# Strassen for the first channel product of eight of nine chunks, with a bank that is seeded by a copy

## The chip, the cores and the metric

The kernel runs on one core of one Trainium2 chip. A core has five engines that run side by side, each through its own instructions in order: TensorE (PE in the profile, its weight loads PEld), VectorE (DVE), ScalarE (ACT), GpSimd (POOL) and SyncE (SP). TensorE multiplies a stationary operand of 128x128 with a moving one and writes into PSUM, eight banks of 128 partitions x 512 float32. DVE and ACT read and write PSUM and the on-chip memory SBUF; POOL works on SBUF alone. DMA queues bring data in and out; POOL's queue also converts types, SP's also transposes. The metric is the device time of one run in microseconds (us).

## The reference

Eight sequences (b) of 576 rows and 8 heads of 64 go through an attention of exponential features, then through a mixer of two products over the rows ("token") and two over the columns ("channel"):

```python
h = x @ omega.T - sum(x*x)/2;  phi = exp(h - max(h)) / sqrt(128)      # for q and k
x = (phi_q @ (phi_k.T @ v)) / (phi_q @ sum(phi_k) + 1e-6)             # per b and head
u = x + (relu(x.T @ w_tok1) @ w_tok2).T                               # 576 -> 256 -> 576
out = u + relu(u @ w_ch1) @ w_ch2                                     # 512 -> 1536 -> 512
```

The matrices on chip are float16, sums are float32, the output is float32.

## The kernel before, in words

The rows of each sequence are split: the first 512 form one chunk, c = 0 to 7, and the last 64 rows of all eight sequences together form chunk 8. Each sequence passes through attention (`attention`), token products (`token_mix`, for the first sequence `token_mix_first`, and `token_tail` for the last rows of two sequences) and a DMA transpose of u to `uT`. Then `channel_mix` works on the chunk. Its first product takes the weights `wc1` (512 x 1536, held as 4 blocks of depth by 12 column blocks) as stationary operand and `uT` as moving one: for each of the 12 column blocks four matmuls of 512 columns into one bank (line 967), and a relu out of the bank into `r3` in float16, by ACT or DVE (lines 290 and 292).

The second product of chunks 1 to 8 is done by Strassen's scheme in Winograd's form (`channel_out_fast`): both factors are cut into 2x2 quarters, and seven products of quarters replace eight. Sums and differences of the weight quarters are made once (`T1` to `T4`, line 448), those of `r3` for each chunk (the sums S, eight DVE instructions of 128x768 a chunk, line 295). The seven products, each 12 matmuls of 256 columns (line 917), accumulate in three banks, X, Y and Z. DVE reads them out (`read`, line 906): the first product (bank X) is read twice in effect, once to u + X into the output tile `o`, and Y is then added to that.

The sequence of everything is fixed. The code makes a list of jobs, each with its engine; `ORDER` says in which order the jobs are issued, `SLOT` which of the rings' buffers or banks each takes, `MOVED` which jobs go to another engine than the usual one. An engine takes its instructions strictly in that order, with semaphores for what it needs from others. Negative entries of `ORDER` are idle matmuls at the start. So attention of later sequences is interleaved by the list with channel products of earlier chunks.

Loads of sequences 2 to 7 go in two steps: POOL's queue casts q and k to float16 into a scratch in DRAM, SP's queue brings them back transposed into rings `qT` and `kT`; v comes by POOL's queue into the ring `v`. Each of these rings has three buffers. POOL otherwise scales v (`vs`, line 295) and the tails of v (`vbd`).

## Time and profile before

| | before |
|---|---|
| time, median of 3 runs | 283.24 us (282.99 to 283.85) |
| span of the profiled execution | 281.1 us |
| TensorE busy | 270.3 us, 96% |
| VectorE busy | 222.4 us, 79% |
| ScalarE busy | 138.6 us, 49% |
| GpSimd busy | 92.0 us, 33% |

The span runs from the first to the last instruction of one profiled execution; the page gives no other time for it. In the rows of groups stand line, engine and operation, the tile written and the tiles read with partitions x elements and type, and how often; behind the bar the busy time in us and the mean length of one in ns, then the idle time of the engine ahead of them with who ended it. Matmuls overlap, so the busy time of PE is more than the time in which its array works; the pitch of a row of matmuls without a gap is read from the chain instead. In the rows of stretches stand the bounds, the length, and the busy time of PE, PEld, DVE, ACT and POOL, with the number of instructions, the granted clock and the share of the DMA engines.

### The profile page before, as it was taken

To read this page: it belongs to the slowest core of one execution; us is meant where nothing else is said; L and a number is where in the kernel's file an instruction comes from. 1 tells how busy PE (TensorE), PEld (TensorE's weight loads), DVE (VectorE), ACT (ScalarE), POOL (GpSimd) and SP (SyncE) were. 2 spreads that over 40 slices of the span, in tenths; PEclk is the share of its full clock that TensorE was granted. 3 is DMA by queue.
4 is the path that set the end of the run, shared out by engine and by line. 5 is a ranking of instruction groups with operands and counts; after the bars stand their busy time and mean duration, and the time that the engine had idled before them with its cause. 6 is when DMAs were issued, how large, how long until landed. Compare 5 with 4: busy or idle time off the path is not lost.

```text
span 281.1 us, 6278 instructions
## 1 busy us (share of the span) xinstructions
PE 270.3 (96%) x2526; PEld 167.6 (60%) x2526; DVE 222.4 (79%) x462; ACT 138.6 (49%) x288; POOL 92.0 (33%) x116
## 2 busy tenths in 40 slices
PE   6899999999999999999999999999999999999993
PEld 2547546443657755665667647755676467446782
DVE  2589828499999899996997999977995893565992
ACT  1498994049676418743758445734753510031200
POOL 8574994007510872048008710510033000000001
PEclk9999999999999999999999999999999999999999
DMA  6999999999998999997979993960151304030125
GB/s 161 194 189 161 157 169 213 178 191 202 179 218 184 148 172 186 181 198 104 212 178 185 241 135 101 161 156 2 76 97 59 111 0 96 0 149 2 75 90 135
DMA packets 80524, 39.66 MB, mean 141 GB/s; under 512 B 63984, under 2 KB 76016, under 8 KB 80304
## 3 DMA queue, kind: packets, MB, share of 16 engines
q0 software_dynamic: 31744, 17.74, 44.1%
q1 hardware_dynamic: 46832, 15.77, 29.1%
q10 hardware_dynamic: 1920, 5.77, 5.4%
q8 instruction: 19, 0.31, 0.4%
q14 instruction: 9, 0.07, 0.1%
HBM read 35.95 MB, written 16.52 MB: 187 GB/s over the span
## 4 chain that ended last, share of the span: by engine, by line
PE 89%; DVE 3%; DMA 2%; ACT 2%; issue 0%; SPq 0%; DVEq 0%
PE bank L967 32%; PE bank L917 26%; PE bank L791 5%; PE bank L778 5%; PE bank L1001 4%; PE bank L735 3%; PE bank L657 3%; PE bank L702 3%; DMA wc<-in_k_dram 2%; PE bank L669 2%; ACT kp L515 1%; PE bank L845 1%; PE bank L817 1%; PE bank L737 1%; PE bank L771 1%; DVE T L448 1%
## 5 line engine op out<-in xcount | busy, mean ns | idle before, releaser
L967 PE MATMUL bank<-uT,wc 128*128 128x512 f16 x376 | 89.6, 379 | 0.5 <-DVE r L292 0.4
L290 ACT ACTIVATE r<-bank 128x512 f16<-128x512 f32 (+1 forms) x86 | 47.7, 601 | 82.7 <-PE bank L967 61.5
L295 POOL TENSOR_TENSOR vs<-v,vs 128x512 f16<-128x512 f16 x32 | 34.2, 1072 | 94.4 <-DVE vs L683 51.3
L967 PEld LDWEIGHTS <-wc 128*128 128x128 f16 x424 | 38.8, 98 | 38.8 <-issue 1.6
L917 PEld LDWEIGHTS <-r 128*128 128x128 f16 x384 | 36.8, 98 | 8.2 <-issue 1.1
L515 ACT ACTIVATE kp<-bank 128x512 f16<-128x512 f32 x64 | 36.7, 618 | 8.9 <-PE bank L657 7.1
L515 ACT ACTIVATE qp<-bank 128x512 f16<-128x512 f32 x64 | 36.7, 614 | 8.8 <-PE bank L669 5.8
L681 DVE TENSOR_REDUCE km<-kp 128x8 f16<-128x1024 f16 x32 | 38.7, 1208 | 1.2 <-ACT kp L515 1.1
L292 DVE TENSOR_SCALAR r<-bank 128x512 f16<-128x512 f32 (+1 forms) x40 | 26.3, 670 | 15.7 <-PE bank L967 11.3
L745 DVE TENSOR_TENSOR x<-bank,rc 128x320 f16<-128x320 f32 x62 | 30.5, 492 | 2.1
L917 PEld LDWEIGHTS <-S 128*128 128x128 f16 x288 | 28.1, 98 | 5.8 <-issue 0.3
L906 DVE TENSOR_TENSOR o<-u,bank 128x512 f32<-128x512 f16 x28 | 19.0, 679 | 6.2 <-PE bank L917 5.8
L917 PE MATMUL bank<-T,r 128*128 128x256 f16 x192 | 23.8, 273 | 0.0
L917 PE MATMUL bank<-wc,r 128*128 128x256 f16 x192 | 23.6, 273 | 0.0
L917 PE MATMUL bank<-T,S 128*128 128x256 f16 x192 | 23.4, 273 | 0.0
L946 POOL DMA_DIRECT2D out_dram<-o x2 | 1.3, 645 | 61.2 <-issue 61.2
L906 DVE TENSOR_TENSOR o<-o,bank 128x512 f32<-128x512 f32 (+1 forms) x27 | 16.6, 617 | 2.5 <-PE bank L917 1.8
L735 PEld LDWEIGHTS <-qp 128*128 128x128 f16 x256 | 13.5, 98 | 8.1 <-DVE kvsb L286 0.7
L794 DVE TENSOR_TENSOR u<-x,bank 128x512 f16<-128x512 f16 x28 | 17.6, 680 | 0.0
L735 PE MATMUL bank<-kvsb,qp 128*128 128x65 f16 x256 | 15.0, 193 | 0.5 <-DVE kvsb L286 0.5
L791 PE MATMUL bank<-r,w 128*128 128x512 f16 x56 | 14.1, 381 | 0.0
L744 DVE RECIPROCAL rc<-bank 128x5 f32<-128x5 f32 x62 | 11.4, 184 | 2.9 <-PE bank L737 2.2
(119 smaller groups left out, 379.0 us busy)
## 6 DMA issues: line engine op xcount, KB each, us to landing
out_dram<-o ACTq DMA_DIRECT2D x9, 512.0 KB, 2.7
q<-in_q_dram POOLq DMA_DIRECT2D x6, 576.0 KB, 9.7
wc<-in_moe_w_ch_dram POOLq DMA_DIRECT2D x4, 768.0 KB, 9.0
k<-in_k_dram POOLq DMA_DIRECT2D x6, 512.0 KB, 7.8
v<-in_v_dram POOLq DMA_DIRECT2D x6, 512.0 KB, 9.9
out_dram<-o SPq DMA_DIRECT2D x5, 512.0 KB, 3.9
r<-in_q_dram POOLq DMA_DIRECT2D x4, 288.0 KB, 7.5
v<-in_v_dram POOLq DMA_DIRECT2D x4, 256.0 KB, 8.1
```

Of the source, the lines that this page charges most:

```text
L290: nc.scalar.activation(out=out, in_=in_, func=AF.Relu)
L292: nc.vector.tensor_relu(out=out, in_=in_)
L295: (nc.gpsimd if eng == "POOL" else nc.vector).tensor_tensor(**kw)
L515: nc.scalar.activation(out=out, in_=in_, func=AF.Exp, bias=0.0, scale=1.0)
L681: nc.vector.reduce_max(out=mx, in_=kpv, axis=AX.X)
L735: nc.tensor.matmul(ps[:, k, j * 65 : (j + 1) * 65], st, s[:, i, 0 : D + 1], start=True, stop=True)
L745: nc.vector.tensor_tensor(out=t_x[place("x", b)][:, :, (2 * hp + hs[0]) * D : (2 * hp + hs[0] + n) * D].rearrange("p j (i d) -> p i j d", ...
L791: nc.tensor.matmul(ps, w2_of(tb, j), r1[:, tb, :], start=(tb == 0), stop=(tb == NT - 1))
L794: nc.vector.tensor_tensor(out=t_u[place("u", b)][:, j, :], in0=t_x[place("x", b)][:, j, :], in1=bank(n), op=ALU.add)
L906: nc.vector.tensor_tensor(out=o, in0=a, in1=ps, op=ALU.add)
L917: nc.tensor.matmul(ps[:, j * DH : (j + 1) * DH], a[:, cb, j * P : (j + 1) * P], w[:, cb, :], start=(bank_of(b, j0) not in held and j == j0 ...
L967: nc.tensor.matmul(ps, wc1[:, db, cb * P : (cb + 1) * P], moving(db), start=(db == 0), stop=(db == ND - 1))
```

## The change

The first channel product of chunks 1 to 8 is done by Strassen's scheme too (`channel_in_fast`). Sums of quarters of `wc1` are made once (`first_weights`: three in a new tile `t_W`, one in place), four sums of quarters of `uT` for each chunk (tile `t_V`, one in place). The 1536 columns are worked in three pairs p of column blocks of both halves. For each pair seven products of four matmuls of 256 columns go into banks X, Y and Z: product 1 into X, then a copy of bank X into bank Y by ACT or DVE, on which product 2 is accumulated; products 6, 7 and 4 go on into X. X is copied out after 6 and after 7 (kept copies `t_s`, float32). Two quarters of the result come straight from a bank with a relu, the other two are the sum of a kept copy and bank Z, written by DVE, and get their relu in place in SBUF (two parts each).

In the second product of chunks 1 to 7, bank X is likewise copied to bank Y behind the first product, and the second is accumulated there; one DVE read falls away per chunk. Matmuls on a seeded bank have no start flag; the list sees to it that the bank's last user wrote all of it.

The rings `qT`, `kT` and `v` go from three buffers to two, `qp` and `kp` from four to three. `T3` and one sum of `wc1` overwrite a quarter of the weights, behind the plain products of chunk 0. `ORDER`, `SLOT` and `MOVED` are new throughout. In them, of the sums S 35 of 64 go to POOL, of the 32 input sums 20, of the eight weight sums three; more jobs have a second engine to choose from. The second product's weights are loaded later, behind the casts of sequence 2.

```diff
-    COUNT = {"qT": 3, "kT": 3, "v": 3, "vt": 2, "qp": 4, "kp": 4, "vs": 4, "qpt": 2, "kpt": 2, "vbd": 2,
-             "kvsb": 3, "ktt": 2, "x": 3, "r1": 3, "u": 3, "uT": 3, "r3": 2, "S": 1, "o": 2, "bank": 8}
+    COUNT = {"qT": 2, "kT": 2, "v": 2, "vt": 2, "qp": 3, "kp": 3, "vs": 4, "qpt": 2, "kpt": 2, "vbd": 2,
+             "kvsb": 3, "ktt": 2, "x": 3, "r1": 3, "u": 3, "uT": 3, "V": 1, "s": 4, "r3": 2, "S": 1, "o": 2, "bank": 8}
...
-    t_T = sb([P, 4, NH, DH], FP16, "T")
+    t_T = sb([P, 3, NH, DH], FP16, "T")
+    t_W = sb([P, 3, 2, NH * P], FP16, "W")
...
+    t_V = ring(COUNT["V"], [P, 3, 2, 2, P], FP16, "V")
+    t_s = ring(COUNT["s"], [P, 512], FP32, "s")
...
+    def second_weights(plain):
+
+        for out_, a, b in ((T1, W12, W11), (T2, W22, T1), (T4, W21, T2), (T3, W22, W12)):
+            e_w = engine("DVE", "POOL")
+            def go_w2(o=out_, a=a, b=b, e_w=e_w):
+                tt(e_w, out=o, in0=a, in1=b, op=ALU.subtract)
+            j_T.append(add(e_w, 0.95, KEYS["T"], go_w2, deps=[*j_wc2, *j_T[-1:], *j_vbd_users, *(plain if b is W12 else [])]))
+
+    A11, A21, A12, A22 = [wc1[:, 2 * k : 2 * k + 2, e * NH * P : (e + 1) * NH * P] for k in range(2) for e in range(2)]
+    S1, S2, S4 = [t_W[:, i] for i in range(3)]
+    S3 = A21
+    j_W = {}
+
+    def first_weights(plain):
+
+        for n, out_, a, b, op in ((1, S1, A21, A22, ALU.add), (2, S2, S1, A11, ALU.subtract), (4, S4, A12, S2, ALU.subtract), (3, S3, A11, A21, ALU.subtract)):
+            e_w = engine("DVE", "POOL")
+            def go_w1(o=out_, a=a, b=b, op=op, e_w=e_w):
+                tt(e_w, out=o, in0=a, in1=b, op=op)
+            j_W[n] = add(e_w, 0.95, KEYS["T"] - 0.2, go_w1, deps=[*j_wc1, *([j_W[n // 2]] if n in (2, 4) else [*j_W.values()]), *(plain if n == 3 else [])])
...
+    PARTS = (slice(0, 4), slice(4, NH))
...
-            prev = []
-            for k, (i, what, op) in enumerate(steps):
-                e_sum = engine("DVE")
-                def go(what=what, op=op, part=part, e_sum=e_sum, c=c, g=g, k=k):
+            for k, (i, what, op, need, after) in enumerate(steps):
+                e_sum = engine("DVE", "POOL")
+                def go_s(what=what, op=op, part=part, e_sum=e_sum, c=c):
                     o, a, b = what()
                     tt(e_sum, out=o[:, part], in0=a[:, part], in1=b[:, part], op=op)
-                job = add(e_sum, 0.5, key + KEYS["S"] + 0.1 * g + 0.01 * k, go, deps=[*need, *prev], take=[("S", c)])
-                prev = [job]
+                job = add(e_sum, (0.61, 0.34)[g], key + KEYS["S"] + 0.1 * g + 0.01 * k, go_s,
+                          deps=[*need, *[sums[x][g] for x in after], *j_early_users], take=[("S", c)])
                 sums.setdefault(i, []).append(job)
...
-                                             start=(bank_of(b, j0) not in held and j == j0 and cb == 0), stop=False, skip_group_check=True)
+                                             start=(bank_of(b, j0) not in held and j == j0 and cb == 0 and (tail or k != 1)), stop=False, skip_group_check=True)
...
-                if k == 0:
+                if k == 0 and tail:
                     outs["sA", h] = read(k, "X", 0, 0, True, [j], False, j0, j1)
+                elif k == 0:
+                    e_a = engine("ACT", "DVE")
+                    def go_a(e_a=e_a):
+                        copy(e_a, bank(bank_of("Y", 0)), bank(bank_of("X", 0)))
+                    outs["sA", h] = add(e_a, 0.5, key + KEYS["c2"], go_a, deps=[j], take=[("bank", bank_of("Y", 0))])
                 elif k == 1:
-                    outs["11", h] = read(k, "Y", 0, 0, False, [j, outs["sA", h]], True, j0, j1)
+                    outs["11", h] = read(k, "Y", 0, 0, not tail, [j, outs["sA", h]], True, j0, j1)
...
+    def channel_in_fast(c, key, jt):
+        def src():
+            return t_uT[place("uT", c)] if c < B else uTt
+        def u_of(k, i):
+            return src()[:, 2 * i : 2 * i + 2, 2 * k : 2 * k + 2, :]
+        def v_of(n):
+            return t_V[place("V", c)][:, n]
+        own = [("uT", c)] if c < B else []
+        first = [tr[x] for x in tr if c < NPE and x[1] == c]
+        sums = {}
+        for n, what, op, after in (
+            (1, lambda: (v_of(0), u_of(0, 1), u_of(0, 0)), ALU.subtract, ()),
+            (2, lambda: (v_of(1), u_of(1, 1), v_of(0)), ALU.subtract, (1,)),
+            (4, lambda: (v_of(2), u_of(1, 0), v_of(1)), ALU.subtract, (2,)),
+            (3, lambda: (u_of(0, 1), u_of(1, 1), u_of(0, 1)), ALU.subtract, (1,)),
+        ):
+            e_sum = engine("POOL", "DVE")
+            def go_u(what=what, op=op, e_sum=e_sum):
+                o, a, b = what()
+                tt(e_sum, out=o, in0=a, in1=b, op=op)
+            sums[n] = add(e_sum, 1.0, key - 0.2, go_u, deps=[*jt, *[sums[x] for x in after]], take=[("V", c)], give=own)
+        ops = {
+            1: ("X", A11, lambda: u_of(0, 0), [], True), 2: ("Y", A12, lambda: u_of(1, 0), [], False),
+            6: ("X", S2, lambda: v_of(1), [sums[2], j_W[2]], False), 5: ("Z", S1, lambda: v_of(0), [sums[1], j_W[1]], True),
+            7: ("X", S3, lambda: u_of(0, 1), [sums[3], j_W[3]], False), 3: ("Z", S4, lambda: u_of(1, 1), [j_W[4]], False),
+            4: ("X", A22, lambda: v_of(2), [sums[4]], False),
+        }
+        raw = {(i, e): [] for i in range(2) for e in range(2)}
+        for p in range(NH // 2):
+            at = key + 0.15 * p
+            def bank_of(b, p=p):
+                return ("c" + b, c, p)
+            def rows(i, e, p=p):
+                return t_r3[place("r3", c)][:, NH * e + 2 * p : NH * e + 2 * p + 2, 2 * P * i : 2 * P * i + 2 * P]
+            def seen(b, bank_of=bank_of):
+                return bank(bank_of(b)).rearrange("p (t s) -> p t s", t=2)
+            def product(n, deps, give=(), p=p, bank_of=bank_of, at=at):
+                b, a, moving, need, begin = ops[n]
+                def go_p(b=b, a=a, moving=moving, begin=begin):
+                    ps, m = bank(bank_of(b)), moving()
+                    for t in range(2):
+                        cb = 2 * p + t
+                        for k in range(2):
+                            nc.tensor.matmul(ps[:, 2 * P * t : 2 * P * t + 2 * P], a[:, k, cb * P : (cb + 1) * P], m[:, :, k, :],
+                                             start=(begin and t == 0 and k == 0), stop=False, skip_group_check=True)
+                j = add("PE", mm(4, 256), at, go_p, deps=[*jt, *j_wc1, *first, *need, *deps], take=[("bank", bank_of(b)), ("r3", c)],
+                        give=[*([("V", c)] if n in (4, 5, 6) else own), *give])
+                j.heavy = True
+                return j
+            def kept(x, deps, give=(), p=p, seen=seen, at=at):
+                e_k = engine("ACT", "DVE")
+                def go_k():
+                    copy(e_k, t_s[place("s", (c, p, x))].rearrange("p (t s) -> p t s", t=2), seen("X"))
+                return add(e_k, 0.5, at, go_k, deps=deps, take=[("s", (c, p, x))], give=give)
+            def summed(x, b, i, e, deps, free, p=p, seen=seen, rows=rows, at=at, bank_of=bank_of):
+                def go_t():
+                    nc.vector.tensor_tensor(out=rows(i, e), in0=t_s[place("s", (c, p, x))].rearrange("p (t s) -> p t s", t=2), in1=seen(b), op=ALU.add)
+                j = add("DVE", 0.6, at, go_t, deps=deps, give=[("s", (c, p, x))] + ([("bank", bank_of(b))] if free else []))
+                raw[i, e].append(j)
+                return j
+            p1 = product(1, [])
+            e_a = engine("ACT", "DVE")
+            def go_a(e_a=e_a, bank_of=bank_of):
+                copy(e_a, bank(bank_of("Y")), bank(bank_of("X")))
+            ka = add(e_a, 0.5, at, go_a, deps=[p1], take=[("bank", bank_of("Y"))])
+            p2 = product(2, [ka])
+            p5 = product(5, [])
+            e_y = engine("ACT", "DVE")
+            def go_y(e_y=e_y, rows=rows, seen=seen):
+                relu_to(e_y, rows(0, 0), seen("Y"))
+            raw[0, 0].append(add(e_y, 0.5, at, go_y, deps=[p2], give=[("bank", bank_of("Y"))]))
+            p6 = product(6, [ka])
+            kb = kept("b", [p6])
+            p7 = product(7, [kb])
+            kc = kept("c", [p7])
+            t22 = summed("c", "Z", 1, 1, [kc, p5], False)
+            p3 = product(3, [t22])
+            summed("b", "Z", 1, 0, [kb, p3], True)
+            p4 = product(4, [kc])
+            e_r = engine("ACT", "DVE")
+            def go_r(e_r=e_r, rows=rows, seen=seen):
+                relu_to(e_r, rows(0, 1), seen("X"))
+            raw[0, 1].append(add(e_r, 0.5, at, go_r, deps=[p4], give=[("bank", bank_of("X"))]))
+        ready = {k: [raw[k][:2], raw[k][2:]] for k in ((0, 0), (0, 1))}
+        for i, e in ((1, 1), (1, 0)):
+            ready[i, e] = []
+            for g, part in enumerate(PARTS):
+                e_p = engine("DVE", "ACT")
+                def go_n(part=part, i=i, e=e, e_p=e_p):
+                    x = t_r3[place("r3", c)][:, NH * e + part.start : NH * e + part.stop, 2 * P * i : 2 * P * i + 2 * P]
+                    relu_to(e_p, x, x)
+                ready[i, e].append([add(e_p, (0.33, 0.2)[g], key + 0.4, go_n, deps=raw[i, e][2 * g : 2 * g + 2])])
+        return ready
...
     def channel_mix(c, key, jt):
+        if c == NPE - 1:
+            first_weights(j_plain["in"])
+            second_weights(j_plain["out"])
+        if c >= NPE - 1:
+            channel_out_fast(c, key, channel_in_fast(c, key, jt))
+            return
         def moving(db):
```

147 lines of the change are left out of this document (81 added, 66 removed), and 110 rows, old and new, of the table ORDER.

## The prediction

> **What bounds the kernel now.** I read the page first, then the busy time by stretch, the chain in order of time, who waited for whom, and last the groups of instructions for prices.
>
> ```profile
> span 281.1 us, 6278 instructions
> PE 270.3 (96%) x2526; PEld 167.6 (60%) x2526; DVE 222.4 (79%) x462; ACT 138.6 (49%) x288; POOL 92.0 (33%) x116
> PE 89%; DVE 3%; DMA 2%; ACT 2%; issue 0%; SPq 0%; DVEq 0%
> DMA  6999999999998999997979993960151304030125
> ```
>
> The median of the runs is 283.24 us, 2.1 us above this span; I count gains in the span and take them off the median. TensorE (PE) holds 89% of the chain. The DMA engines are full up to about slice 26 (183 us).
>
> ```profile
> 67.00:281.10 214.10, 208.57 (x1868) 133.89 (x1864) 176.59 (x360) 97.29 (x197) 52.29 (x61) 1.00 0.68 127
> 67.00:209.00 142.00, 141.59 (x1363) 89.89 (x1360) 127.99 (x264) 83.70 (x171) 47.01 (x56) 1.00 0.90 157
> 67.00:95.00 28.00, 27.59 (x277) 17.72 (x274) 26.33 (x52) 19.14 (x40) 9.45 (x12) 1.00 1.04 182
> PE bank L967 <- DVE r L292: 0.4, 1, 0.4
> PE bank L771 <- DVE x L745: 0.3, 1, 0.3
> ```
>
> Chunk 1's first product begins near 67 us. The first three rows give, after the length, busy PE, weight loads, DVE, ACT and POOL; from there to the end PE is covered, and the last two rows are all that it waited for (0.7 us). DVE is busy 127.99 of 142 us (90%) up to 209 us and 26.33 of 28 (94%) in the fullest stretch, still without holding PE up. So two limits lie close together: PE, which the change unloads, and DVE, which it loads.
>
> **The change part by part. PE.**
>
> ```profile
> 229.29 5.24 PE bank L917 x48
> 238.88 13.81 PE bank L967 x64
> L917 PEld LDWEIGHTS <-r 128*128 128x128 f16 x384 | 36.8, 98 | 8.2 <-issue 1.1
> ```
>
> Back to back, a 512-column matmul of the first product takes 13.81/64 = 215.8 ns, and a 256-column one, the form that all new products have, 5.24/48 = 109.2 ns. A chunk's first product goes from 48 x 0.2158 = 10.36 us to 84 x 0.1092 = 9.17 us: 1.19 us, for eight chunks 9.5 us. The bank copy adds nothing on PE. The weight load of 98 ns still fits under 109. In the Trainium skill, "TensorE: Matmul & The Clock Gate", section "Back-to-back issue gap", a sustained stream is put at about 81 ns for 128 columns and 131 ns for 512; by that (an estimate, 98 ns for 256 columns) the plain form would take 6.3 us and the new one 8.2, a loss. The rows above contradict it at both widths, and the rows decide.
>
> **DVE, ACT and POOL.** Prices (mean ns in the second place behind the bar):
>
> ```profile
> L290 ACT ACTIVATE r<-bank 128x512 f16<-128x512 f32 (+1 forms) x86 | 47.7, 601 | 82.7 <-PE bank L967 61.5 <-PE bank L778 11.4 <-DVE o L906 5.4
> L292 DVE TENSOR_SCALAR r<-bank 128x512 f16<-128x512 f32 (+1 forms) x40 | 26.3, 670 | 15.7 <-PE bank L967 11.3 <-PE bank L778 3.6 <-PE bank L552 0.5
> L906 DVE TENSOR_TENSOR o<-o,bank 128x512 f32<-128x512 f32 (+1 forms) x27 | 16.6, 617 | 2.5 <-PE bank L917 1.8 <-issue 0.3
> L286 DVE COPY o<-bank 128x512 f32<-128x512 f32 x2 | 1.4, 686 | 0.2 <-PE bank L1001 0.2
> L286 ACT COPY o<-bank 128x512 f32<-128x512 f32 x2 | 1.2, 602 | 1.4 <-PE bank L1001 1.4
> L295 DVE TENSOR_TENSOR S<-r 128x768 f16<-128x768 f16 x16 | 8.8, 551 | 0.6 <-ACT r L290 0.4
> L295 POOL TENSOR_TENSOR vs<-v,vs 128x512 f16<-128x512 f16 x32 | 34.2, 1072 | 94.4 <-DVE vs L683 51.3 <-PE bank L669 22.2 <-PE bank L917 13.8
> L295 POOL TENSOR_TENSOR vbd<-vt,vbd 128x512 f16<-128x512 f16 x6 | 6.3, 1053 | 20.4 <-DVE vbd L594 17.7 <-DMA vt<-in_v_dram 2.6
> L295 POOL TENSOR_TENSOR T<-vt,T 128x1024 f16<-128x1024 f16 x1 | 1.9, 1937 | 0.0
> 20.22 1.07 POOL L295 TENSOR_TENSOR vs<-v,vs 128x512 f16<-128x512 f16 x1
> 20.62 0.83 DVE L631 COPY qpt<-qpt 128x512 f16<-128x512 f16 x1 [0.49 <-ACT qpt L515]
> 64.51 0.91 DVE L448 TENSOR_TENSOR T<-wc,T 128x1536 f16<-128x1536 f16 x1
> 64.85 1.48 POOL L295 TENSOR_TENSOR vs<-v,vs 128x512 f16<-128x512 f16 x1
> 65.33 1.81 DVE L448 TENSOR_TENSOR T<-wc 128x1536 f16<-128x1536 f16 x1
> 71.05 1.07 POOL L295 TENSOR_TENSOR vs<-v,vs 128x512 f16<-128x512 f16 x1
> 71.13 1.82 DVE L448 TENSOR_TENSOR T<-wc,T 128x1536 f16<-128x1536 f16 x1
> ```
>
> I counted the jobs of both lists by engine (the order in which the code makes jobs, with the table of moved ones). DVE loses 35 of 64 sums S (x 0.551 = 19.3 us), 20 of 40 relus out of a bank (x 0.670 = 13.4), 7 reads of the second product (x 0.617 = 4.3) and six small copies (0.3 to 0.8 each, 4.3): 41.3 us. It gains 48 sums of a kept product and a bank (nearest row L906, 0.617): 29.6; 13 bank or kept copies (0.686): 8.9; 12 sums of 512 elements over the chunk's input, by the slope from 768 elements at 0.551 to 1536 at 0.91, 0.43 each: 5.2; 17 in-place relus; a fifth weight sum, 0.9; and five value products from POOL, 2.4. For an in-place relu the nearest row is the copy within SBUF at 20.62: 0.83 us, of which it stood 0.67 behind a POOL product that ended at 21.29, so 0.16 alone. Between 0.16 and 0.83 I take 0.3, since half its length was standing still and the first parts are twice as long: 5.1. Net 52.1 - 41.3 = +11 us, nearly all behind 67 us: 176.6 + 11 = 188 us.
>
> ACT gains 27 bank copies and 39 kept copies (x 0.602 = 39.7), loses 28 relus (x 0.601 = 16.8) and gets 15 in-place relus (0.6 for 512 elements, up to 1.0): some 13. From 138.6 us to about 175, 64% of the new span: never the bound, but now four times in the bank X of every product pair. The list puts at least 0.8 us of other PE work between a product and the next that needs its copy (the least of 24 pairs; the middle ones have 1.3 to 3.3), against a copy of 0.60. I cost the bank copies at nothing, covered by that work; without cover each would cost PE 0.6 us. A product that waits for its copy holds every later group in PE's queue, attention's too, and the copy stands in ACT's queue behind the exponentials. Behind the last attention only channel products are left; there chunks 7 and 8 cover each other's copies, at least 0.87 us in the list.
>
> POOL gains 35 sums S (17 of 1024 elements x 1.937, 18 of 512 x 1.072), 20 input sums (1.072) and three weight sums (1.5 x 1.937 each): 82 us, so about 170 with what it hands over, 63%. Work on two operands is then 119 us, 44% of the new span. POOL's queue also issues all casting loads, so a load now stands behind sums that wait for the transposed input.
>
> What DVE and POOL do to each other is the unknown. Where two such instructions meet in the rows above, one stands still: the weight sum alone took 0.91 us, and 1.81 and 1.82 beside a POOL product; the product at 64.85 took 1.48 and not 1.07. The Trainium skill says it so in "SBUF — State Buffer", section "Who interferes with whom": a VectorE instruction with two SBUF inputs, or in a two-port mode, and a GpSimd instruction that reads SBUF hold a shared port, and the loser blocks fully. The trace agrees: 0.9 us lost by DVE per meeting. It speaks against the change, which puts far more of both kinds on these engines.
>
> ```profile
> L295 DVE TENSOR_TENSOR S<-r x16: 547/551/559, 80.7 to 266.5; 128x768 f16<-128x768 f16 x16
> ```
>
> (Minimum, median, maximum: the sums S never met one; by chance about 64 x 16% = 10 would have, POOL's products of before being 32 x 1.072 + 6 x 1.053 + 2 x 1.94 = 44.5 us of 281.) After the change 68 DVE instructions are of this kind. DVE standing still holds the reads that free banks, and PE behind them. At random 44% of them, 30, would start inside a POOL sum and stand for half of its mean 1.28 us: 19 us. Laid apart as S was, none. I take a third, 6 us, nearer to the row that shows none, but there is less room to lie apart: 188 + 6 = 194 us on DVE. Filled to 93%, about what the fullest stretch shows, that takes 208.6 us where PE alone needs 214.1 - 9.5 = 204.6. So DVE decides: gain 5.5 us.
>
> **Loads.** Rings for q, k and v shrink from three to two.
>
> ```profile
> 175.54 3.23 SPq L380 DMA_TRANSPOSE kT<-k  x1
> 202.16 0.62 PE L657 MATMUL bank<-omT,kT 64*128 64x128 f16 x16
> 60.55 0.12 PEld L552 LDWEIGHTS <-kT 64*128 64x128 f16 x4 [0.48 <-DMA kT<-k]
> q0 software_dynamic: 31744, 17.74, 44.1%
> wc<-in_moe_w_ch_dram POOLq DMA_DIRECT2D x4, 768.0 KB, 9.0
> kT<-k SPq DMA_TRANSPOSE x6, 6.8
> ```
>
> The last batch's k is fetched 26 us ahead of its main use: two buffers at a distance of a chunk (142 us over five, about 28) suffice and cost nothing; with that cover gone each batch would wait up to the 6.8 us of a transpose. Batch 2 is different. PE waited for it already (0.48 us), and the new list puts it 18 us of PE work earlier. Ahead of it the second product's weights (two loads of 768 KB) have gone; at the casting queue's 17.74 MB in 183 us they are worth 16 us. It comes 2 us late, or at the outside between 2 us early and 4 late; since PE's part before it also has gaps to give, I take 1 us. The head's other reordering, the new slots and the store queues moved from SP to ACT (their issue is not on the chain) I cost at nothing, inside the same bounds. The tail's stores are as before.
>
> Sum: 283.24 - 5.5 + 1.0 = 278.7 us.
>
> **The rivals.** *Full gain*: sums and POOL work lie apart, DVE 188/0.93 = 202 us stays under PE's 204.6: 283.24 - 9.5 = 273.7. For it: 0.7 us of PE waits with DVE at 90%. Against it: POOL's share goes from 16% to 44%.
>
> *DVE and POOL in each other's way, slower*: the random 19 us gives (188 + 19)/0.93 = 222.6, 8.5 us more than 214.1: 291.7. It tips to slower from about 12 us of standing still: (188 + 12)/0.93 = 215. For it: three of the four weight sums met a product, two stood still. Against it: S, none of 64.
>
> *Loads late*: batch 2, or a cast held up in POOL's queue, keeps PE waiting 10 us instead of 1: 283.24 - 9.5 + 10 + the 1 to 2 us of a jammed restart, 285.
>
> *Narrow matmuls slower than wide ones per column*, by the TensorE page's figures 283.24 + 8 x 1.9 = 298 (an estimate from that page). As a mechanism of rows: 84 weight loads x 98 ns = 8.2 us, under 9.17, so loads do not bind. Chance under 1 in 100.
>
> **How the numbers follow.** Below 275.5, full gain and a head that gets shorter: 0.17. The forecast, 275.5 to 282.4: 0.42. Within 0.3%, about what a measurement of this kernel can tell from no change (282.4 to 284.1): 0.05. DVE and POOL: 0.26. Loads or head late: 0.10. Hence faster 0.59, same 0.05, slower 0.36. The likeliest case by itself spans 275.5 to 282; the range reaches to 272.5, the full gain with a us from the head, and to 290, most of the slower cases.
>
> **What would show it.** Steps right: the first product's line gives way to 84 matmuls of 256 columns per chunk at 109 ns; DVE near 188 us behind 67 us plus what its SBUF sums grew by; PE waiting some 4 us for DVE, in rows that name sums, kept copies or the in-place relus. Sums S on DVE with a maximum far above their median show meetings, and their excess is the 6 us. A wait of PE for kT near batch 2 shows the load term. It is wrong if those sums stay at their median and PE waits for nothing (full gain), if their excess passes 12 us, or if PE waits for bank copies by ACT, which I put at nothing.

## The result and the profile after

The change makes the kernel slower: 298.78 us in the median of four runs (296.59 to 300.26) against 283.55 us (282.99 to 284.21) before, a ratio of 1.052 with a 95% interval of 1.046 to 1.058. The forecast was 278.7 us, with a range to 290.0: the time lies outside it, on the side of the rival "DVE and POOL in each other's way", and 7 us beyond that rival's own 291.7. Ratios here leave disturbed runs out, so a ratio need not be that of two medians. The profiled execution of after has a span of 298.3 us, 17.2 more than before.

The head of the page of after, then the chain by engine, the granted clock and the share of the DMA engines in 40 slices:

```profile
span 298.3 us, 7029 instructions
PE 272.9 (91%) x2814; PEld 199.3 (67%) x2814; DVE 248.5 (83%) x490; ACT 172.3 (58%) x347; POOL 177.8 (60%) x168
PEclk9975999979999999999999799999999999999997
DMA  7999999999999798999987729390360034300124
PE 60%; DVE 17%; DMA 9%; POOL 5%; issue 4%; ACT 3%; DVEq 0%; POOLq 0%
```

PE falls from 89% to 60% of the chain; DVE has 17% and transfers 9%. Next the stretches of before, then of after, cut where chunk 1's first product begins (65 us, where the prediction reads 67, and 77 us); behind the length stand busy PE, weight loads, DVE, ACT and POOL, then the clock and the DMA share. In the table of after, the third row is the stretch in which the clock is lowest, and the fourth the stretch from 67 us for which the prediction made its DVE sum.

```profile
0.00:65.00 65.00, 59.69 (x651) 32.95 (x652) 43.85 (x102) 39.32 (x89) 37.70 (x54) 1.00 1.15 182
65.00:281.10 216.10, 210.57 (x1877) 134.66 (x1876) 178.59 (x361) 99.29 (x201) 54.29 (x63) 1.00 0.68 129
```

```profile
0.00:77.00 77.00, 67.60 (x715) 38.04 (x716) 53.74 (x118) 46.38 (x103) 47.38 (x58) 0.91 1.12 175
77.00:298.30 221.30, 205.26 (x2103) 161.29 (x2101) 194.80 (x373) 125.91 (x246) 130.46 (x110) 0.99 0.65 119
20.00:30.00 10.00, 8.85 (x138) 6.52 (x136) 6.49 (x18) 8.63 (x23) 7.00 (x10) 0.55 1.15 167
67.00:298.30 231.30, 215.26 (x2209) 166.97 (x2207) 200.56 (x385) 130.17 (x254) 135.57 (x113) 0.99 0.67 119
```

Idle PE (length less busy) is 5.3 us ahead of the cut and 5.5 behind it before, 9.4 and 16.0 after: 14.6 of the 17.2 us; the other 2.6 us are busy time. That PE is busier although its products need less hides more loss: stalls shorter than a matmul's modelled end, and a slow clock, count as busy. So I also counted gaps from the start of each matmul to the start of the next, less the pitch of its form at full clock. They come to 30.7 us before (18.0 ahead of the cut, 12.7 behind) and 56.3 after (27.5 and 28.8). The 9.5 us saved less 25.6 us of added gaps leave 16.1 us lost, close to the 17.2. So two costs have to be found, 9.5 us in the head, which here means all ahead of the cut, and 16.1 behind it.

What PE waited for behind the cut, after (before, the two rows shown in the prediction hold all of it, 0.7 us), and the longest waits in the head that before does not have:

```profile
PE bank L952 <- DVE S L309: 3.3, 3, 2.7
PE bank L1042 <- DMA uT<-u: 1.9, 1, 1.9
PE bank L952 <- DVE o L941: 1.9, 2, 1.2
PE bank L825 <- DVE r L1055: 1.4, 1, 1.4
PE bank L689 <- DVE ut L886: 0.7, 1, 0.7
PE bank L1042 <- DVE r L1055: 0.4, 1, 0.4
PE bank L1042 <- ACT bank L300: 0.3, 1, 0.3
```

```profile
PE bank L1141 <- DMA wc<-in_moe_w_ch_dram: 1.8, 1, 1.8
PE bank L734 <- ACT qp L547: 1.1, 1, 1.1
PE bank L520 <- DMA r<-in_q_dram: 1.1, 1, 1.1
PE bank L651 <- DVE qT L300: 0.8, 1, 0.8
```

DVE stands in five of the seven rows behind the cut; a bank copy (ACT bank) cost 0.3 us. The next two views show where DVE's time went. First, of after, one row each (count; minimum, median and maximum in ns; first and last start) of the lines of the sums and of the relus:

```profile
L309 DVE TENSOR_TENSOR S<-S,r x8: 417/684/4731, 92.0 to 284.8; 128x1024 f16<-128x1024 f16 x4, 128x512 f16<-128x512 f16 x4
L306 DVE TENSOR_SCALAR r<-r x17: 241/416/2056, 85.6 to 281.4; 128x1024 f16<-128x1024 f16 x10, 128x512 f16<-128x512 f16 x7
```

Then the timeline around 160 us (start, length), of DVE and behind it of POOL:

```profile
159.68 0.42 DVE L309 TENSOR_TENSOR r<-r 128x512 f16<-128x512 f16 x1
160.02 4.73 DVE L309 TENSOR_TENSOR S<-S,r 128x512 f16<-128x512 f16 x1
```

```profile
158.49 1.15 POOL L309 TENSOR_TENSOR S<-r 128x512 f16<-128x512 f16 x1 [3.95 <-ACT r L304]
160.26 2.13 POOL L309 TENSOR_TENSOR r<-r 128x1024 f16<-128x1024 f16 x1
162.34 2.12 POOL L309 TENSOR_TENSOR S<-r,S 128x1024 f16<-128x1024 f16 x1
```

A DVE sum of 512 elements that takes 0.42 us took 4.73: it ended 0.3 us behind the second of two POOL sums that follow each other without a break, and PE's longest wait for S, 2.67 us, ended just behind it, at 164.81 us. Added over all DVE instructions with two operands in SBUF or in place, each against the shortest of its shape, DVE has an excess of 17.4 us in after and 2.5 in before, POOL 12.9 and 1.0.

Not all of this excess is standing still. Plain sums and products with a repeated operand have the same shape and take different times even alone: for 512 elements 0.42 and 0.68 us on DVE, 1.15 and 1.05 us on POOL. Held against the shortest of its own kind, DVE stood 15.6 us in after and POOL 6.0. Fifteen DVE instructions lost more than 0.15 us each, 13.2 us together, and the one above is a third of that. The excesses named below are by shape.

### The profile page after: what moved, and what is told of

It is laid out like the page before. It is cut to its first block, busy times and chain, and to the rows that moved or that the text cites. A ratio compares the mean times of both kernels' runs of the same rounds, so it can differ in the third digit from the quotient of the medians.

```text
span 298.3 us, 7029 instructions
## 1 busy us (share of the span) xinstructions
PE 272.9 (91%) x2814; PEld 199.3 (67%) x2814; DVE 248.5 (83%) x490; ACT 172.3 (58%) x347; POOL 177.8 (60%) x168
## 4 chain that ended last, share of the span: by engine, by line
PE 60%; DVE 17%; DMA 9%; POOL 5%; issue 4%; ACT 3%; DVEq 0%; POOLq 0%
PE bank L1042 19%; PE bank L952 18%; PE bank L1141 4%; DMA wc<-in_moe_w_ch_dram 4%; DMA uT<-u 4%; DVE S L309 3%; PE bank L825 3%; DVE km L713 3%; PE bank L734 2%; PE bank L812 2%; PE bank L769 2%; DMA r<-in_q_dram 2%; PE bank L689 2%; PE bank L701 2%; DVE o L941 2%
## 5 line engine op out<-in xcount | busy, mean ns | idle before, releaser
L304 ACT ACTIVATE r<-bank 128x512 f16<-128x512 f32 (+1 forms) x58 | 33.6, 606 | 14.7 <-PE bank L1042 11.5
L1042 PE MATMUL bank<-uT,wc 128*128 128x256 f16 x252 | 34.9, 272 | 2.4 <-DMA uT<-u 1.9
L952 PE MATMUL bank<-wc,r 128*128 128x256 f16 x288 | 35.6, 273 | 1.2 <-DVE o L941 1.2
L1055 DVE TENSOR_TENSOR r<-s,bank 128x512 f16<-128x512 f32 x48 | 32.1, 678 | 2.7 <-PE bank L1042 1.2
L300 ACT COPY s<-bank 128x512 f32<-128x512 f32 x39 | 22.2, 594 | 19.2 <-PE bank L1042 13.5
L1042 PEld LDWEIGHTS <-W 128*128 128x128 f16 x288 | 26.8, 98 | 5.2 <-issue 0.8
L300 ACT COPY bank<-bank 128x512 f32<-128x512 f32 x27 | 15.5, 586 | 22.3 <-PE bank L1042 20.8
L1042 PE MATMUL bank<-V,W 128*128 128x256 f16 x192 | 27.0, 273 | 0.0
L309 POOL TENSOR_TENSOR S<-r,S 128x1024 f16<-128x1024 f16 (+1 forms) x11 | 19.0, 1730 | 7.2 <-DVE S L309 7.1
L309 POOL TENSOR_TENSOR S<-S,r 128x512 f16<-128x512 f16 (+1 forms) x8 | 13.6, 1695 | 10.9 <-DVE S L309 10.7
```

What stands on the lines that cost most here:

```text
L300: (nc.scalar.copy if eng == "ACT" else nc.vector.tensor_copy)(out=out, in_=in_)
L304: nc.scalar.activation(out=out, in_=in_, func=AF.Relu)
L309: (nc.gpsimd if eng == "POOL" else nc.vector).tensor_tensor(**kw)
L952: nc.tensor.matmul(ps[:, j * DH : (j + 1) * DH], a[:, cb, j * P : (j + 1) * P], w[:, cb, :], start=(bank_of(b, j0) not in held and j == j0 ...
L1042: nc.tensor.matmul(ps[:, 2 * P * t : 2 * P * t + 2 * P], a[:, k, cb * P : (cb + 1) * P], m[:, :, k, :], start=(begin and t == 0 and k == 0 ...
L1055: nc.vector.tensor_tensor(out=rows(i, e), in0=t_s[place("s", (c, p, x))].rearrange("p (t s) -> p t s", t=2), in1=seen(b), op=ALU.add)
```

## The experiments

Every kernel was timed beside the one of before. Numbers are ratios to it with their 95% intervals; the changed kernel has 1.052 (1.046 to 1.058), and one per cent is 2.8 us.

### DVE and POOL

**POOL's sums as fills.**

```diff
-                    tt(e_sum, out=o[:, part], in0=a[:, part], in1=b[:, part], op=op)
+                    if e_sum == "POOL":
+                        nc.gpsimd.memset(o[:, part], 0.0)
+                    else:
+                        tt(e_sum, out=o[:, part], in0=a[:, part], in1=b[:, part], op=op)
...
-                tt(e_sum, out=o, in0=a, in1=b, op=op)
+                if e_sum == "POOL":
+                    nc.gpsimd.memset(o, 0.0)
+                else:
+                    tt(e_sum, out=o, in0=a, in1=b, op=op)
```

> POOL's 35 sums S and its 13 input sums V are replaced by fills of the same targets with zeros, on POOL, at the same places of the list; the numbers of these sums are left out of the computation. A fill reads no operand. Theory 'standing still' (DVE stood 17.4 us beyond the shortest length of each form, POOL 12.9): DVE's excess falls to about 4 us (what is left are meetings with the value products and weight sums on POOL), PE's waits for S go, and the time falls by 8 to 12 us, to 287 to 291. Theory 'head and loads' (most of the loss lies before 80 us: late second-product weights, cold TensorE clock): at most 3 us fall, 296 or more, because these sums begin only behind 77 us. Since fills are also shorter than sums, the gain is an upper bound for what the standing still costs.

The input sums on POOL are 20, not 13. Ratio 1.031 (1.024 to 1.038), profiled span 289.6 us. The four runs lie far apart (291.38 to 301.53 us), so the size of the gain is uncertain. DVE's excess falls to 10.3 us, no sum S on DVE takes over 0.95 us, and PE waits for no S. Both theories get about half: some 6 us, less than the 8 to 12. The maximum of the sums is the point: a fill reads no operand, and no DVE sum that overlaps one takes longer than it does alone (0.69 us at most; the sum of 0.95 us stands beside a product of POOL). The Trainium skill says so in "SBUF — State Buffer", section "Who interferes with whom": a DVE instruction with two SBUF inputs contends with a GpSimd instruction that reads SBUF and not with one that only writes. The trace agrees for the sums: 4.73 us at most beside POOL's sums, 0.69 beside its fills. The in-place relus do stand beside fills. This one, which takes 0.41 us alone, ended 0.3 us behind two fills in a row (DVE's row, then POOL's):

```profile
200.19 1.96 DVE L306 TENSOR_SCALAR r<-r 128x1024 f16<-128x1024 f16 x1
```

```profile
200.03 1.84 POOL L914 MEMSET S<- 128x1024 f16 x2
```

Five relus beside fills lost 3.1 us. So the fills do not take all the standing still away, and the gain is not the upper bound that was expected of it.

**Eight sums S moved to DVE**, those beside which the longest standing still is seen.

```diff
 MOVED = {
-654: "POOL", 656: "POOL", 816: "POOL",
...
-1378: "POOL", 1379: "POOL", 1380: "POOL", 1381: "POOL", 1382: "POOL",
+654: "DVE", 656: "DVE", 816: "DVE",
...
+1378: "DVE", 1379: "DVE", 1380: "DVE", 1381: "DVE", 1382: "DVE",
```

> Eight of POOL's sums S go to DVE, those beside which the longest standing still of DVE is seen: two of chunk 3 (1024 elements, back to back at 160.26 and 162.34 us, while DVE's 512-element sum from 160.02 took 4.73 us), one of chunk 4 (207.22, beside the in-place relu of 1.91 us), all five of chunk 8 (281.4 to 287.4). DVE gains 4 x 0.68 + 4 x 0.43 = 4.4 us of work and loses 4.3 + 1.5 + 0.8 + 1.0 = 7.6 us of standing still. Theory 'standing still': PE's wait of 2.84 us for S at 164.8 us and some 1 us of waits behind 283 us go, 3 to 4 us faster than the changed kernel, 295 to 296. Rival 'DVE is simply full': the 4.4 us of added work fill what is won, within 1 us of 298.8.

Ratio 1.029 (1.023 to 1.035), 292.64 us in the median: 6 us faster, more than the 3 to 4 expected, though DVE has 4.4 us more to do. The rows of this run that answer to those above, of the sums' line and of the stretch behind the cut:

```profile
L309 DVE TENSOR_TENSOR S<-S,r x9: 415/425/693, 90.5 to 276.9; 128x512 f16<-128x512 f16 x5, 128x1024 f16<-128x1024 f16 x4
```

```profile
75.70:289.70 214.00, 203.53 (x2103) 160.66 (x2101) 190.54 (x381) 125.81 (x246) 116.25 (x102) 0.99 0.64 123
```

The 4.73 us are gone, DVE's excess is 10.6 us, the losses of more than 0.15 us add up to 6.1 us instead of 13.2, and behind the cut 221.3 us have become 214.0. Gaps of PE there fall from 28.8 to 21.4 us. It is the clearest evidence that standing still costs time, and the best kernel of the study; it is still slower than before.

**All 35 sums S to DVE.**

```diff
 MOVED = {
-331: "POOL", 332: "POOL", 335: "POOL", 336: "POOL", 337: "POOL",
...
+331: "DVE", 332: "DVE", 335: "DVE", 336: "DVE", 337: "DVE",
...
```

> All 35 sums S that POOL has go to DVE; POOL keeps 13 input sums, the value products and three weight sums. DVE gains 17 x 0.68 + 18 x 0.42 = 19.1 us of work. Moving eight of them gave 6.2 us. Theory 'meetings decide' (no sum S on POOL, so DVE's excess falls from 17.4 us to about 4): further gain, 288 to 292. Rival 'load decides once the worst meetings are gone': DVE at 248.5 + 19.1 - 13 = 255 us, over 90% of the span behind 77 us, and PE waits for it: slower than with eight moved, 294 to 300.

(POOL keeps 20 input sums, as above.) Ratio 1.070 (1.063 to 1.077), slower than the changed kernel. The rival is right: DVE is busy 204.28 of 224 us (91%), and what PE waits for is no longer the sums but everything behind them on DVE. The stretch, and two rows of the waits:

```profile
76.00:300.00 224.00, 207.52 (x2115) 162.34 (x2113) 204.28 (x411) 127.55 (x248) 72.28 (x75) 1.00 0.62 118
```

```profile
PE bank L952 <- DVE o L941: 2.7, 4, 1.4
PE bank L1042 <- DVE r L1055: 1.4, 3, 0.6
```

So the sums can't be on POOL for the meetings, nor all on DVE for the load.

**Three more neighbours moved.**

```diff
 MOVED = {
+444: "DVE", 538: "DVE", 874: "DVE",
```

> Three more of POOL's two-operand instructions go to DVE beside the eight sums S: the value products vs 3.0 and vs 5.1 and one input sum of chunk 2, next to which DVE's input sum took 1.37 us at 107.3 and its in-place relu 2.06 us at 148.1 us in the run with eight moved. DVE gains 3 x 0.42 = 1.3 us and loses 1.0 + 1.65 of standing still. Theory 'standing still, place by place': PE's wait of 1.4 us behind 150 us (token mixing of batch 4, for the sum that stands behind that relu) goes: 1 to 2 us below 292.6. Rival: next to nothing, within 0.7 us, since other DVE work takes the place.

Ratio 1.029 (1.024 to 1.034): no gain. The wait of 1.4 us is gone as the theory has it, but in its place this run shows PE waiting 1.9 us for uT at 138 us, as the changed kernel does and the run with eight moved does not. So a wait of 2 us can appear with an edit that does not touch it, and steps smaller than that can't be told here.

**Only the sums S on POOL, in the kernel of before.**

```diff
 MOVED = {
+301: "POOL", 302: "POOL", 305: "POOL", 306: "POOL", 307: "POOL",
...
```

> The kernel of before with one thing of the change alone: the 35 sums S that the changed kernel gives to POOL are given to POOL here too (same chunks and numbers, here 768 elements each), all else as before; the list stays. DVE loses 35 x 0.551 = 19.3 us, POOL gains 35 sums of about 1.6 us = 56 us. Theory 'DVE and POOL in each other's way': though DVE is relieved, its excess over the shortest lengths rises from 2.5 us to 10 or more, POOL's sums are late for the products that need them, and the time is 4 to 12 us above before. Rival: the relief outweighs it, within 1 us of before.

Ratio 1.064 (1.057 to 1.070), 302.85 us: 18 us slower with nothing else of the change, more than the 4 to 12 expected. The rows of its sums and of PE's waits:

```profile
L296 POOL TENSOR_TENSOR S<-r,S x11: 1632/1639/1952, 120.6 to 289.2; 128x768 f16<-128x768 f16 x11
L296 DVE TENSOR_TENSOR r<-r x7: 551/1974/1993, 148.0 to 281.8; 128x768 f16<-128x768 f16 x7
```

```profile
PE bank L918 <- POOL S L296: 7.5, 4, 2.6
PE bank L658 <- DVE o L907: 2.6, 1, 2.6
```

The median of seven DVE sums is 1.97 us where the shortest is 0.55; before, the maximum of all 64 was 0.56. DVE's excess rises from 2.5 to 12.8 us, and PE waits 7.5 us for sums that POOL makes three times as slowly (1.64 against 0.55 us). This list was not planned for it, so the 18 us are no estimate of the cost in a planned one; but the change's list was, and still shows 17.4 us of excess. Nor does the run part the two costs that it shows, DVE standing still and PE waiting for POOL's slower sums.

**In-place relus to ACT, and shortened.**

```diff
 MOVED = {
...
+327: "ACT", 328: "ACT", 329: "ACT", 330: "ACT",
...
+490: "ACT",
...
```

> The 17 in-place relus that DVE has go to ACT, at the same places of the list. DVE loses 10 x 0.78 + 7 x 0.28 = 9.7 us of busy time, meetings included; ACT gains about 10 x 1.04 + 7 x 0.61 = 15 us, to about 187 us (63%). Theory 'DVE decides behind 67 us': the time falls by some 6 to 9 us, to 290 to 293. Rival 'DVE is full on paper only, single waits decide': within 2 us of 298.8; or slower, if ACT's longer relus (1.04 for 0.41 us) now hold the sums S that wait for them.

(All 17 relus are moved in this way.) Ratio 1.066 (1.060 to 1.071), slower: the rival's second half. On ACT a relu of 1024 elements takes 1060 ns and one of 512 takes 644, against 407 and 241 at the least on DVE; PE waits 1.7 us for ACT's relus and 1.6 for its kept copies. In the second run the relus stay on DVE and are cut to 8 of the 256 columns of each group:

```diff
+                    if e_p == "DVE":
+                        x = x[:, :, 0:8]
                     relu_to(e_p, x, x)
```

> The 17 in-place relus that DVE has act on 8 of 256 columns of each group alone; the rest of these two blocks isn't clipped. DVE loses about 10 x 0.7 + 7 x 0.2 = 8.5 us, ACT and POOL keep their work. Theory 'DVE decides behind 77 us, by load as much as by meetings': 6 to 9 us faster than the changed kernel, 290 to 293 (moving the relus to ACT gave no gain, since ACT's longer relus held the sums S). Rival 'single meetings and loads decide': 1 to 3 us faster, the wait beside the relu at 152.8 us alone.

Ratio 1.037 (1.031 to 1.044): 4 us, between the two theories. The same sum as before still took 4.74 us and PE still waited 2.7 us for it. The relus' busy time fell by 5.1 us (from 9.4 to 4.3), less than the 8.5 expected, since the shortened relus still stand beside POOL (1.66 us the longest, 0.12 the shortest). So DVE's load behind the cut counts, at most of its length.

### The head and the loads

**Warm clock.** Fourteen matmuls of zeros into idle banks.

```diff
 ORDER = [
...
+-3, -3, -3,
...
+-2, -2, -2, -2,
...
+-4, -4, -4, -4, -4, -4, -4,
```

> Fourteen matmuls of zeros are added on PE into idle banks at places where it waits in the head: 3 ahead of batch 0's q tail (16.0 us), 4 ahead of the first key-value product (17.97 us), 7 ahead of the first second-product matmul of chunk 0 (59 us). They compute nothing that is used. Theory 'cold clock' (granted clock 0.88, 0.50 and 0.60 in the three stretches of 5 us from 15 us, 0.77 from 60 to 67): the clock stays near 1.00 there, PE's 8.9 us busy from 20 to 30 us shrink to about 6, and the time falls by 2 to 4 us, to 295 to 297. Rival 'loads set the head': the clock rises but the first product of chunk 1 still begins near 77 us, and the time stays within 1 us.

The clock does what was expected, and the time does not follow: ratio 1.055 (1.052 to 1.059). This run's stretch from 20 to 30 us and its one long wait behind the cut:

```profile
20.00:30.00 10.00, 7.90 (x153) 5.72 (x153) 7.91 (x22) 9.88 (x28) 7.34 (x10) 1.00 1.11 166
```

```profile
PE bank L727 <- POOL vbd L295: 4.9, 1, 4.9
```

Chunk 1's first product begins 3 us earlier, and a wait of 4.9 us for batch 3's tail value operand takes it back. With eight sums moved as well:

> The eight sums S of the longest meetings on DVE and the fourteen added matmuls together, full loads. Theory 'loads give it back': the time stays within 1 us of the 292.6 of the moved sums alone. Rival 'the clock is a cost of its own': the 3 us of the head stay, 289 to 290.

Ratio 1.032 (1.023 to 1.041), with eight sums alone 1.029: nothing gained again. Chunk 1's first product begins at 74.5 us, where it begins at 75.7 with the eight sums alone, and behind that PE waits 2.1 and 1.7 us for kT.

**Second product's weights earlier.**

```diff
 ORDER = [
...
+42, 41,
 273,
...
-42,
...
-41,
```

> The two loads of the second product's weights move in POOL's queue from behind the value products vs to ahead of the first weight sum (issue at about 38 us, not 46 to 48). Theory 'head and loads': PE's wait of 2.0 us for these weights at 59 us goes and the clock behind it (0.77 from 60 to 67 us) stays near 1.00: 2 to 3.5 us faster, 295 to 297. Rival: the part behind 80 us is bound by DVE and swallows it, or another load becomes late by the same amount: within 1 us of 298.8.

Far off: ratio 1.112 (1.107 to 1.117), 17 us slower than the changed kernel. The transposes of batch 2 in the timeline of SP's queue, first in the changed kernel, then in this one; then the loads in POOL's timeline and PE's waits here:

```profile
39.83 4.17 SPq L394 DMA_TRANSPOSE kT<-k  x1
44.05 2.58 SPq L394 DMA_TRANSPOSE qT<-q  x1
```

```profile
39.91 11.06 SPq L380 DMA_TRANSPOSE kT<-k  x1
51.02 12.51 SPq L380 DMA_TRANSPOSE qT<-q  x1
```

```profile
38.92 1.66 POOL L1146 DMA_DIRECT2D wc<-in_moe_w_ch_dram  x2
```

```profile
PE bank L570 <- DMA kT<-k: 13.6, 1, 13.6
PE bank L687 <- DMA qT<-q: 3.2, 1, 3.2
```

Issued one us ahead of the transposes, the two loads of 768 KB stretch them from 6.8 to 23.6 us together. The late weights in the changed list are thus the smaller evil: 1.8 us of wait against 16.8 for kT and qT.

**Rings.** The kernel of before with the smaller rings alone.

```diff
-    COUNT = {"qT": 3, "kT": 3, "v": 3, "vt": 2, "qp": 4, "kp": 4, "vs": 4, "qpt": 2, "kpt": 2, "vbd": 2,
+    COUNT = {"qT": 2, "kT": 2, "v": 2, "vt": 2, "qp": 3, "kp": 3, "vs": 4, "qpt": 2, "kpt": 2, "vbd": 2,
```

> The kernel of before, with the buffer counts of the changed one alone: q, k and v two buffers, not three, the exponentials kp and qp three, not four. The list stays, but a job that finds no buffer is put off until there is one. The prediction put the rings of q, k and v at nothing and doesn't price those of kp and qp. Theory 'the rings cost the head': 3 to 10 us slower than before, 287 to 293, with new gaps of PE ahead of 65 us that name kp and qp's readers. Rival 'the rings are free': within 1 us of before.

Ratio 1.082 (1.072 to 1.091), 23 us slower. The list runs out of kp and qp buffers in the attention of every batch (replayed on the list, 16 jobs find no kp or qp buffer at their place and 37 more wait behind those, while for q, k and v a single job is put off), and PE waits for the exponentials that then come late, 13.9 us in all with two smaller rows:

```profile
PE bank L958 <- ACT qp L506: 4.3, 5, 1.3
PE bank L726 <- ACT qp L506: 2.7, 4, 1.2
PE bank L693 <- ACT kp L506: 2.6, 3, 1.2
PE bank L958 <- ACT kp L506: 2.4, 4, 0.7
```

A list planned for three buffers does better, as the changed one shows; what the run shows is that with three the order of before isn't to be had. (A later expectation puts these waits at 19 us; the rows come to 13.9.)

**The list of before for the head**, put in front of the changed one: first with three buffers, then with four for kp and qp, then that with the eight sums moved. The diff has the counts of the second and third; the new `ORDER` of the head isn't shown.

```diff
-    COUNT = {"qT": 2, "kT": 2, "v": 2, "vt": 2, "qp": 3, "kp": 3, "vs": 4, "qpt": 2, "kpt": 2, "vbd": 2,
-             "kvsb": 3, "ktt": 2, "x": 3, "r1": 3, "u": 3, "uT": 3, "V": 1, "s": 4, "r3": 2, "S": 1, "o": 2, "bank": 8}
+    COUNT = {"qT": 2, "kT": 2, "v": 2, "vt": 2, "qp": 4, "kp": 4, "vs": 4, "qpt": 2, "kpt": 2, "vbd": 2,
+             "kvsb": 3, "ktt": 2, "x": 3, "r1": 3, "u": 2, "uT": 2, "V": 1, "s": 4, "r3": 2, "S": 1, "o": 2, "bank": 8}
...
```

> The changed kernel with the list of before up to the first matmul of chunk 1's first product, as far as the smaller rings allow it (three buffers each for the exponentials kp and qp, not four: a job that finds no buffer is put off until there is one); the weight sums stand as early as their inputs allow, and behind it follows the list of after. Theory 'the list of the head costs it' (PE has 27.5 us of gaps ahead of chunk 1's first product, before 18.0): that product begins near 68 us, not 77, and the time falls by 5 to 9 us, to 290 to 294. Rival 'the rings cost it' (with three buffers the order of before isn't to be had any more, the attention of batch 0 waits for buffers, and the loads of batch 2 come too late for the list that follows): no gain, or up to 10 us slower.

> The changed kernel with the whole list of before up to the first matmul of chunk 1's first product, nothing put off: the exponentials kp and qp have four buffers again, paid for with one buffer each of u and of its transposed form (two, not three, which the list never needs). The weight sums W stand behind the last load of batch 2, and from the cut on the list of after follows. Theory 'list and rings of the head cost it' (27.5 us of PE gaps ahead of chunk 1's first product, before 18.0; in the run with the smaller rings alone the kernel of before lost 23 us and PE waited 19 us for kp and qp): the first product of chunk 1 begins 5 to 9 us earlier than in the changed kernel, near 68 to 72 us, and the time is 290 to 294. Rival 'the loads decide and only move': the head gets shorter, but transfers of batches 3 and 4, which the second half of the list expects earlier, become late and PE waits for them: within 2 us of 298.8 or slower.

> The two last edits together: the head of before with four buffers for kp and qp, and the eight sums S of the longest meetings on DVE. If the two costs are separate, as the theory has it, the gains add: about 6.2 us below the run with the head alone, 284 to 288. If the loads of batches 3 and 4 become late, the sum is less, and the waits name kT, qT or vt.

Three buffers: 1.123 (1.114 to 1.132), the rival, but not by the rings alone: I had put the first weight sums right behind their loads, so POOL stood 8.4 us for the load, DVE 12.1 us for POOL's sum, and PE 12.2 us for a relu queued behind on DVE. With four buffers and these sums further back: 1.056 (1.049 to 1.064); with the eight sums: 1.045 (1.039 to 1.051). The head is mended up to 67 us (chunk 0's second product ends at 67.3 us, not 76.1; the gaps up to there are 20.6 us), and then it is given back. Where the two lists meet, PE waits (run with the head alone):

```profile
PE bank L742 <- DVE vs L317: 5.9, 2, 5.1
```

Batch 2's value products stand on DVE behind two weight sums, and the list has no product to put ahead of them. **Seam mended** (277 to 279 are the weight sums T1, T2 and T4, 406 a value product of batch 2 and 393 its first key-value product; the eight numbers ahead of 393 are chunk 1's products 1 and 2 with their bank copies and relus):

```diff
 ORDER = [
...
-277,
...
-278,
 406,
+277, 278, 279,
...
-279,
+285, 286, 299, 300, 287, 289, 301, 303,
 393,
...
```

> The last kernel (head of before with four buffers for kp and qp, eight sums S on DVE) with its seam mended: DVE's weight sums T stand behind the value products of batch 2, not ahead of them, and the first two products of two thirds of chunk 1 stand in PE's queue ahead of batch 2's first key-value product, where PE waited 5.4 + 1.0 + 0.7 us at 71.5 to 74.1 us. Theory 'the head's gain was given back at the seam': these 7 us go, 288 to 291, which is below the 292.6 of the eight moved sums alone, and the head's gaps are shown to be the list's. Rival 'the loads of batches 3 and 4 bound it': PE waits for kT, v or vt between 75 and 105 us instead, 294 to 297.

Ratio 1.046 (1.040 to 1.051): no gain, 297.33 us. The wait of 5.9 us is gone, and in its place PE waits 3.2 us for a bank that an exponential of qp still holds, 2.0 for an input sum and 2.1 for kT of batch 4. None of the four tries to join the head of before to the list of after brought a gain.

**Lighter loads**, in the changed kernel, in the one of before, and with the warm clock.

```diff
+                n8 = P if b < 3 else 8
...
-                    out=scratch[w, b].rearrange("(p r) e -> p (r e)", p=P),
+                    out=scratch[w, b].rearrange("(p r) e -> p (r e)", p=P)[0:n8],
...
-                nc.sync.dma_start_transpose(out=t.unsqueeze(1), in_=scratch[w, b])
+                nc.sync.dma_start_transpose(out=t.unsqueeze(1), in_=scratch[w, 2])
```

> The casting loads of q and k for batches 3 to 7 move one sixteenth of their bytes (8 of 128 rows of the copy, one of 16 row groups), and the transposes read batch 2's copy instead: about 5 MB less traffic, every DMA still issued at its place. The attention of batches 3 to 7 is thus computed from batch 2's q and k. Theory 'loads give back what the head gains' (transposes on SP take 2.6 to 8.1 us in the changed kernel, and the late uT at 139 us and the second product's weights at 59 us are transfers behind others): the transposes fall to about 3 us, these two waits of 2.0 us and part of the gaps ahead of 77 us go: 294 to 297. Rival 'the head is a chain of engines, not of transfers': within 1 us of 298.8.

> The same lighter loads in the kernel of before. PE waits there for DMA only in the first 10 us (1.6 us for the first keys) and 0.2 us for kT. Theory: no gain, within 1 us of before, so that what the light loads save in the changed kernel is the change's own cost. Rival: DMA binds before as well, 2 us or more faster.

> The light loads and the fourteen added matmuls of zeros together. The added matmuls alone held the clock at 1.00 and brought chunk 1's first product from 77.0 to 74.0 us, but PE then waited 5.0 us for batch 3's tail value operand at 97 us, whose load had been issued at 79 to 81 us beside a transpose of 7.9 us. Theory 'loads give it back': with light loads the 3 us stay, so 2 to 3 us below the light loads alone, 291 to 294. Rival: something else than transfers holds that operand, and the time stays that of the light loads alone.

Ratios 1.046 (1.041 to 1.051), 1.001 (0.998 to 1.004) and 1.043 (1.038 to 1.048). The first lies at the edge of the changed kernel's interval. PE's wait for uT is gone in it, but its wait for the sums S has risen from 3.3 to 4.5 us and that for the second product's weights is still 1.9:

```profile
PE bank L954 <- DVE S L309: 4.5, 3, 2.7
PE bank L1143 <- DMA wc<-in_moe_w_ch_dram: 1.9, 1, 1.9
```

So the loads of q and k for batches 3 to 7 are some 2 us of the loss, by the two intervals at most 4. Those of batch 2 and of the weights, on which the head depends, were left as they are.

The run with the warm clock doesn't test whether loads give the head's gain back, because its head gains nothing: in the profiled execution the clock fell to 0.66 from 20 to 25 us in spite of the added matmuls, and chunk 1's first product began at 77.6 us. PE's wait for batch 3's tail value operand is 0.6 us there, not 4.9. The question stays open.

## Why the prediction was wrong

**PE's part was right.** The pitch holds: in the tail of after, where nothing stops PE, the starts of groups of four and eight matmuls of the new first product lie 0.44 and 0.87 us apart, 109 ns each.

```profile
254.48 1.04 PE L1042 MATMUL bank<-uT,wc 128*128 128x256 f16 x8
255.35 0.60 PE L1042 MATMUL bank<-V,W 128*128 128x256 f16 x4
255.79 1.04 PE L1042 MATMUL bank<-uT,wc 128*128 128x256 f16 x8
```

The saving of 9.5 us is made, and swallowed. Bank copies at nothing was right as well: they take 586 ns in the mean, and PE waited 0.3 us for one.

**DVE's and POOL's work was about right.** Behind 67 us DVE was forecast at 188 us plus what its sums grow by; it is busy 200.56, of which 15 to 16 are standing still, so about 185 of work. ACT was put at about 175 and has 172.3, POOL at about 170 and has 177.8, its own standing still included. The in-place relu, priced at 0.3 us, has 0.24 and 0.41 as its shortest.

**"I take a third, 6 us" is the step that failed first.** DVE's excess is 17.4 us by shape and 15.6 by kind of instruction, well past the 12 us that the prediction itself named as a sign of being wrong. It is near the 19 us of the random count, but that is luck in part: fifteen instructions lost 0.9 us each in the mean, where the random count has thirty that lose 0.64. The sums S of before, which met nothing, were no guide: there no product of POOL met them; with 132 us of two-operand work on POOL (forecast 119) some do. And the price of a meeting was drawn too small: half a POOL sum in the mean, whereas behind two sums in a row DVE waited for both.

By the prediction's own formula 16 us give (188 + 16)/0.93 = 219 us for that stretch, 5 us more than the 214.1 of before, where the forecast had 5.5 us less. PE waits 8.3 us for DVE in the rows above and their smaller fellows, not "some 4". The rival with this mechanism was named, with the right point of tipping, and had 0.26. The runs support it: 6 us came back with eight sums moved, and the kernel of before lost 18 us with S on POOL alone, though POOL's slower sums have a part in that. Of the 16.1 us behind the cut, these 6 are the part that an experiment traces to the meetings; how the rest divides between further meetings and DVE's fuller load isn't shown.

**"The head's other reordering ... I cost at nothing" is the second.** PE's gaps ahead of chunk 1's first product grew by 9.5 us. The prediction priced the rings of q, k and v, rightly at nothing, and left out those of kp and qp, four buffers to three, which stand in the same line of the diff. They are what takes the order of before away. How much of the 9.5 us they cost in a list planned for them isn't shown: in the changed kernel PE's waits for exponentials in the head come to 1.6 us, and the list of before for the head brings its gaps back near the 18 us of before, but every attempt gave that back at 70 to 100 us. The clock of 0.55 between 20 and 30 us has a part in the head: with the added matmuls, which held it at 1.00, chunk 1's first product began 3 us earlier. It explains none of the time, since a later wait took the 3 us.

The load term, 1 us, came out near by luck and not by its mechanism. It was to be a wait for batch 2's keys; PE waits for no transfer of them. It waits 1.8 us for the second product's weights, which the new list loads later to make room for batch 2, and 1.9 for uT at 138 us.

**"Loads late"** looked at the head, where a loss was, but named the wrong cause, and **"full gain"** falls with the first step.

What stays open: whether a list planned as a whole with four kp and qp buffers (there is room, since u and its transposed form need two each, not three) and with few sums on POOL would win the 9.5 us back. It wasn't tried, as it needs the planner that made the lists. No kernel here is faster than before; the best, with eight sums moved, stays 2.9% behind.

## What to carry to other kernels

Before work is moved from a full VectorE to an idle GpSimd, count how many of both engines' instructions have two operands in SBUF or work in place: the idle engine is not free, and one meeting can cost the length of two of its instructions, not half of one. Read a ring's size in the diff as part of the order of work, all rings of the line, and ask which order it no longer allows. A saving on the bounding engine is worth what the engine behind it leaves, and here the forecast itself had the two 2% apart (208.6 and 204.6 us).

## What the runs showed of the hardware

- A DVE sum waited through two POOL sums in a row (4.73 us for 0.42), in nearly the same length in every run that kept these two: 4.73 to 4.75 us in nine runs. POOL went on from one instruction to the next without DVE getting in between.
- Fills on POOL held up no DVE sum (0.69 us at most beside them), but they held up DVE's in-place relus: 1.96 us behind two fills for 0.41.
- Transposes on SP's queue were stretched by casting loads issued one us ahead of them on POOL's: 4.17 and 2.58 us became 11.06 and 12.51.
- The granted clock fell to 0.50 from 20 to 25 us of the changed kernel while PE was busy 2.99 of the 5 us before and 4.46 of those 5. Fourteen idle matmuls more held it at 1.00 in two runs, without a gain in the time; in a third, with lighter loads, it still fell to 0.66.
- POOL's sums of 1024 elements take 2.12 us and those of 512 take 1.15, where its products with a repeated operand take 1.92 and 1.05 (median). On DVE the same sums take 0.68 and 0.42.
